# Gate and up as nine pairs of half-height matmuls in a two-layer SSM and GEGLU kernel

## The chip, the cores and the metric

The kernel runs on one core of a Trainium2 chip. The metric is device time in microseconds (us) for one execution; the time given for a kernel is the median of its runs. The engines are named as the profile names them: PE is TensorE (matmul; its weight loads are listed as PEld), DVE is VectorE, ACT is ScalarE, POOL is GpSimd and SP is SyncE, which issues most of the DMAs.

## The reference

The sequence x has 2048 rows of 576 channels (bf16). Two layers are applied, each made of a gated long convolution A and a feed-forward block B, both with a residual:

```
def _A_ref(q, k, v, shift_k, ssm_k, ssm_D):      # q is the normalised x
    kv = shift_conv(k, shift_k) * v              # 4 taps along the sequence
    y  = long_conv(kv, ssm_k) + kv * ssm_D       # causal, length 2048, by FFT
    return q * y
def _B_ref(x, w_gate, w_up, w_down):             # 576 -> 4608 -> 576
    return (_gelu(x @ w_gate) * (x @ w_up)) @ w_down

x = A_q
x = x + _A_ref(_layernorm(x), A_k, A_v, ...)
x = x + _B_ref(_layernorm(x), ...)
x = x + _A_ref(_layernorm(x), A_k, A_v, ...)
x = x + _B_ref(_layernorm(x), ...)
```

k, v and the filters are the same in both layers, so y is computed once. Only the normalisation, the product with y, and the feed-forward block are done per layer.

## The kernel before

The first part (function `ssm_phase_A`, lines 71 to 256) computes y by block-wise Fourier transforms on TensorE. Its filter transposes (L145) take five pieces of the 576 channels: four of 128 rows and one of 64.

The second part (`ssm_geglu_kernel`) holds the feed-forward block, and it is where the change is. The 2048 rows are cut into four chunks of CH = 512 rows, each of STC = 4 row tiles of 128. A *unit* is one chunk in one layer; L361 lists the eight units, all four chunks of layer 0 and then all four of layer 1. The hidden 4608 columns are cut into FT = 36 steps of 128, in nine groups of FG = 4 that share weight tiles. All weights stay in SBUF once loaded: group 0 is loaded in the first part (`load_w`, L325), groups 1 to 8 when the first part's buffers are free.

A unit, in the order in which it is written out (L434 on):

- `ln_finish` (L387) has transposed the normalised chunk: per block of 128 channels four transposes (L400) into a PSUM tile, then a copy to SBUF on DVE (L401). 576 is 4 x 128 + 64. The first four blocks serve gate and up alike. For the last 64 channels there are two extra blocks, `xnT_rA` with the 64 channels in its lower rows (rows 0 to 63) and zeros above, and `xnT_rB` with zeros below and the channels in its upper rows (64 to 127). The tile `wr` holds the last 64 rows of the gate weights in its lower half and those of up in its upper half, so a matmul of full height with `rA` gives gate's rest and one with `rB` gives up's.
- `gate_up(f)` (L438) runs five matmuls of 128 rows and 512 columns for gate into the PSUM tile pg, and then five for up into pu (L444, L447).
- `act_mul` (L451) applies GELU to pg on ACT (L453) and multiplies with pu on DVE (L455), which gives hT.
- `down(f)` (L458) multiplies hT with the down weights: for each of four row tiles one matmul of 512 columns (L461) and one of 64 (L464), accumulated in five PSUM banks (acc) over all 36 steps.

PSUM has three tiles (psum_gu, L357) for pg, pu and the transposes, which take turns, and one set of acc tiles. The text writes gate_up(f+1) ahead of down(f), so TensorE goes gate_up(f), down(f-1), gate_up(f+1), down(f).

Work for later units is hung into the steps as tasks (L468 on): the product with y for the next layer's or the next chunk's rows (`gate_A1_st`, `_gate_residual` L271), the normalisation of the next unit's chunk (`ln_st`, L372), and at last `ln_finish` for it. The residual additions (L413, L415) end a unit. All chunks of x are loaded to SBUF in float32 through POOL's queue ahead of the loop (L421), and stay there.

The framework's planner takes the instructions in this order, with costs of its own, lets an engine go on with a later instruction that is ready when the next one isn't, and fixes each engine's order before the kernel runs; on the chip each engine keeps to its list. It also sets the semaphores.

Of the kernel before, what the change touches and what calls it, by code (L numbers as in the profile page):

```python
# [11 lines left out]
ALU = mybir.AluOpType  # L12
F32 = mybir.dt.float32
BF16 = mybir.dt.bfloat16
# [3 lines left out]
P = 128  # L18
# [264 lines left out]
def ssm_geglu_kernel(ctx, tc, A_q, A_k, A_v, A_shift_k, A_ssm_k, A_ssm_D, B_x, B_w_gate, B_w_up,  # L283
                     B_w_down, out, debug=None):
    nc = tc.nc
    q2 = A_q[0]
    out2 = out[0]
    S, D = q2.shape
    F = B_w_gate.shape[1]
    NST = S // P  # L290
    CH = 512
    NCH = S // CH
    STC = CH // P
# [4 lines left out]
    NDTF = D // P  # L298
    DREM = D - NDTF * P
# [2 lines left out]
    DR = D - DM  # L302
    assert STC * DR <= 512
    EPS = 1e-5
    XW = D + (2 * DREM if DREM else 0)
# [7 lines left out]
    neghalf_t = persist.tile([P, 1], F32, name="neghalf_t")  # L313
    nc.vector.memset(neghalf_t[:], -0.5)

    wg, wu, wr, wd = {}, {}, {}, {}
    fw = FG * P

    def alloc_w(pool, g):
        wg[g] = pool.tile([P, NDTF, fw], BF16, name=f"wg{g}")  # L320
        wu[g] = pool.tile([P, NDTF, fw], BF16, name=f"wu{g}")
        wr[g] = pool.tile([P, fw], BF16, name=f"wr{g}") if DREM else None
        wd[g] = pool.tile([P, FG, D], BF16, name=f"wd{g}")

    def load_w(g):  # L325
        f0 = g * fw
        nc.sync.dma_start(out=wg[g][:], in_=B_w_gate[0:NDTF * P, f0:f0 + fw].rearrange("(dt p) f -> p dt f", p=P))
        nc.sync.dma_start(out=wu[g][:], in_=B_w_up[0:NDTF * P, f0:f0 + fw].rearrange("(dt p) f -> p dt f", p=P))
        if DREM:
            nc.sync.dma_start(out=wr[g][0:DREM, :], in_=B_w_gate[NDTF * P:D, f0:f0 + fw])  # L330
            nc.sync.dma_start(out=wr[g][DREM:2 * DREM, :], in_=B_w_up[NDTF * P:D, f0:f0 + fw])
        nc.sync.dma_start(out=wd[g][:], in_=B_w_down[f0:f0 + fw, :].rearrange("(ft p) d -> p ft d", p=P))

    pre = ctx.enter_context(tc.tile_pool(name="pre", bufs=1))
# [5 lines left out]
        return  # L340

    xc0pool = ctx.enter_context(tc.tile_pool(name="xc0", bufs=1))
    x_c = [xc0pool.tile([P, STC, D], F32, name="x_c0")]
# [4 lines left out]
    for c in range(1, NCH):  # L348
        x_c.append(xrpool.tile([P, STC, D], F32, name=f"x_c{c}"))
# [16 lines left out]
    def ln_begin(c):  # L366
        stt = LNState()
        stt.c = c
        stt.xns = [None] * STC
        return stt  # L370

    def ln_st(stt, j):  # L372
        st = stt.c * STC + j
        mv = small.tile([P, 2], F32, tag="mv")
        rstd = small.tile([P, 1], F32, tag="rstd")
        _ln_stats(nc, small, xs(st), D, eps_t, neghalf_t, mv[:], rstd[:], "l_")
        xn = xnp.tile([P, XW], BF16, tag=f"xn{j}", bufs=1)
        nc.vector.tensor_scalar(out=xn[:, 0:D], in0=xs(st), scalar1=mv[:, 0:1],
                                scalar2=rstd[:, 0:1], op0=ALU.subtract, op1=ALU.mult)
        if DREM:  # L380
            nc.gpsimd.memset(xn[:, D:D + DREM], 0.0)
            nc.vector.tensor_scalar(out=xn[:, D + DREM:XW], in0=xs(st)[:, D - DREM:D],
                                    scalar1=mv[:, 0:1], scalar2=rstd[:, 0:1],
                                    op0=ALU.subtract, op1=ALU.mult)
        stt.xns[j] = xn

    def ln_finish(stt):  # L387
        xns = stt.xns
        xnT = xnp.tile([P, NDTF, CH], BF16, tag="xnT")
        xnT_rA = xnT_rB = None  # L390
        blocks = [(dt * P, xnT[:, dt, :]) for dt in range(NDTF)]
        if DREM:
            xnT_rA = xnp.tile([P, CH], BF16, tag="xnT_rA", name="xnT_rA")
            xnT_rB = xnp.tile([P, CH], BF16, tag="xnT_rB", name="xnT_rB")
            blocks.append((NDTF * P, xnT_rA[:]))
            blocks.append((NDTF * P + DREM, xnT_rB[:]))
        for (c0, dst) in blocks:
            pt = psum_gu.tile([P, CH], BF16, tag="gu")
            for j in range(STC):
                nc.tensor.transpose(out=pt[:, j * P:(j + 1) * P], in_=xns[j][:, c0:c0 + P], identity=ident[:])  # L400
            nc.vector.tensor_copy(out=dst, in_=pt[:])  # L401
        return xnT, xnT_rA, xnT_rB

    def residual_adds(layer, c, acc):
        last_layer = layer == NLAYER - 1
# [11 lines left out]
            if last_layer:  # L417
                nc.sync.dma_start(out=out2[st * P:(st + 1) * P, :], in_=ob[:])

    for c in range(NCH):  # L420
        nc.gpsimd.dma_start(out=x_c[c][:],  # L421
                            in_=q2[c * CH:(c + 1) * CH, :].rearrange("(st p) d -> p st d", p=P))
    for j in range(STC):
        gate_A1_st(j)
    wpool = ctx.enter_context(tc.tile_pool(name="weights", bufs=1))
    for g in range(1, NFG):
        alloc_w(wpool, g)
        load_w(g)
    st0 = ln_begin(units[0][1])
    for j in range(STC):  # L430
        ln_st(st0, j)
    cur = ln_finish(st0)
    pending = []
    for ui, (layer, c) in enumerate(units):  # L434
        xnT, xnT_rA, xnT_rB = cur
        acc = psum_acc.tile([P, STC + (1 if DR else 0), 512], F32, tag="acc")

        def gate_up(f):  # L438
            g, fi = divmod(f, FG)
            pg = psum_gu.tile([P, CH], F32, tag="gu")  # L440
            pu = psum_gu.tile([P, CH], F32, tag="gu")
            for (pd, wm, rr) in ((pg, wg[g], xnT_rA), (pu, wu[g], xnT_rB)):
                for dt in range(NDTF):
                    nc.tensor.matmul(pd[:], lhsT=wm[:, dt, fi * P:(fi + 1) * P], rhs=xnT[:, dt, :],  # L444
                                     start=(dt == 0), stop=(dt == NDTF - 1 and not DREM))
                if DREM:
                    nc.tensor.matmul(pd[:], lhsT=wr[g][:, fi * P:(fi + 1) * P], rhs=rr[:],  # L447
                                     start=False, stop=True)
            return pg, pu

        def act_mul(pg, pu):  # L451
# [23 lines left out]
        if ui + 1 < len(units):  # L475
            nlayer, ncu = units[ui + 1]
            assert ncu != c or NCH == 1
            if ncu != c:
                nxt_state = ln_begin(ncu)
                fslot = max(fslot, 6)  # L480
                for j in range(STC):
                    if nlayer == 0:
                        tasks.setdefault(min(fslot, FT - 1), []).append(lambda j=j, ncu=ncu: gate_A1_st(ncu * STC + j))
                        fslot += 1
                    tasks.setdefault(min(fslot, FT - 1), []).append(lambda j=j, stt=nxt_state: ln_st(stt, j))
                    fslot += 1
                tasks.setdefault(min(fslot, FT - 1), []).append("finish")
# [25 lines left out]
        cur = nxt_cur  # L513
# [50 lines left out]
```

## Time and profile before

| What | Value |
|---|---|
| Median of three runs | 1129.36 us (1128.77 to 1131.19) |
| Profiled execution: span, first to last instruction | 1127.3 us |
| Between this span and the median | 2.1 us |
| PE busy | 96% of the span, 6464 matmuls |
| DVE busy | 45% |
| ACT busy | 24% |
| Mean granted TensorE clock | 0.986 |
| First matmul of the feed-forward part | 202.3 us |

The page gives the profiled execution by its span, and no other time of its own; what lies around it is worked out against the median. In the timeline each row gives the start, the length, the engine, the source line, the operation with its output and inputs, the shape of the array used (rows*columns, as 128*128) and that of the data, and how many instructions were merged in the row. Matmuls are pipelined: a row's length is longer than the slot that the matmul takes from the next, so slots are read from start to start. A time in brackets is idle time of the engine ahead of the row, with what ended it.

### The profile page before, as it was taken

The page shows a single profiled execution, that of the slowest core. Times are in us where ns is not written, and L with a number is a line of the kernel's source. Part 1 is how long each engine was busy: PE and PEld are TensorE (multiplying, and loading weights), DVE is VectorE, ACT ScalarE, POOL GpSimd, SP SyncE. Part 2 cuts the span into 40 slices and gives each one's busy share as a digit, 9 for nine tenths or more (in the row PEclk, how much of TensorE's full clock was granted, in tenths as well). Part 3 has the DMA queues.
Part 4 walks back from the last instruction along what each step waited for, and adds up shares of the span by engine and source line. Part 5 has one row for each costly group of instructions (what it writes and reads, how often), then busy time and mean ns, then how long its engine had stood idle before and what let it go on. Part 6 is the DMA issues. An engine that isn't in the chain of part 4 may idle for free.

```text
span 1127.3 us, 15633 instructions
## 1 busy us (share of the span) xinstructions
PE 1080.8 (96%) x6464; PEld 519.2 (46%) x6464; DVE 507.0 (45%) x1072; ACT 265.8 (24%) x503; POOL 53.0 (5%) x111
## 2 busy tenths in 40 slices
PE   5999994999999999999999999999999999999997
PEld 1544433444444444444444444444444444444443
DVE  5947999722276226942652255323232322232222
ACT  5875211111111111111111111111111111111111
POOL 0001002100011001200100000000000000000000
PEclk9999997899999999999999999999999999999999
DMA  7921004950000000000000000000000000000000
GB/s 221 293 75 43 1 1 116 339 175 1 1 1 1 1 1 1 1 1 1 1 1 1 1 1 1 1 1 22 1 1 1 22 1 1 1 22 1 1 1 22
DMA packets 33654, 38.73 MB, mean 34 GB/s; under 512 B 1845, under 2 KB 31408, under 8 KB 33584
## 3 DMA queue, kind: packets, MB, share of 16 engines
q1 hardware_dynamic: 31472, 33.03, 9.8%
q0 software_dynamic: 2112, 4.72, 1.4%
q8 instruction: 50, 0.82, 0.3%
q14 instruction: 20, 0.16, 0.0%
HBM read 33.02 MB, written 2.36 MB: 31 GB/s over the span
## 4 chain that ended last, share of the span: by engine, by line
PE 82%; DVE 11%; issue 3%; DMA 1%; ACT 1%; POOL 1%; SPq 1%; DVEq 0%; ACTq 0%; POOLq 0%
PE acc L461 21%; PE pg L444 20%; PE pu L444 20%; PE pg L447 5%; PE pu L447 5%; PE ps L134 3%; PE acc L464 3%; DVE pr L231 2%; PE ps L254 2%; DVE stats L264 2%; PE Yps L235 1%; DVE hT L455 1%; PE pt L400 1%; DVE t L276 1%; POOL rstd L268 1%
## 5 line engine op out<-in xcount | busy, mean ns | idle before, releaser
L455 DVE TENSOR_TENSOR hT<-ga,pu 128x512 bf16<-128x512 f32 x288 | 197.4, 686 | 558.7 <-PE pu L447 557.5
L453 ACT ACTIVATE ga<-pg 128x512 f32<-128x512 f32 x288 | 171.9, 597 | 740.3 <-PE pg L447 730.1
L461 PEld LDWEIGHTS <-hT 128*128 128x128 bf16 x1152 | 112.7, 98 | 138.9 <-DVE hT L455 6.3
L464 PEld LDWEIGHTS <-hT 128*128 128x128 bf16 x1152 | 112.9, 98 | 32.1
L268 POOL TENSOR_TENSOR rstd<-ve,neghalf_t 128x1 f32<-128x1 f32 x64 | 44.2, 696 | 372.3 <-DVE ve L267 370.5
L134 PEld LDWEIGHTS <-GF 128*128 128x128 bf16 x512 | 35.2, 101 | 49.9 <-issue 20.1
L134 PE MATMUL ps<-hT_blk,GF 128*128 128x512 bf16 (+1 forms) x256 | 38.9, 311 | 11.4 <-ACT Hf_0_237 L137 4.8
L235 PE MATMUL Yps<-pr,ident 128*128 128x512 bf16 (+1 forms) x180 | 45.7, 330 | 1.7 <-DVE pr L231 0.7
L254 PE MATMUL ps<-zb,GI 128*128 128x512 bf16 (+1 forms) x192 | 34.4, 289 | 6.9 <-DVE zb L245 3.8
L461 PE MATMUL acc<-wd_2381,hT 128*128 128x512 bf16 x128 | 36.8, 380 | 1.0 <-DVE hT L455 1.0
L461 PE MATMUL acc<-wd_2390,hT 128*128 128x512 bf16 x128 | 36.5, 380 | 0.0
L461 PE MATMUL acc<-wd_2372,hT 128*128 128x512 bf16 x128 | 35.7, 380 | 0.0
L461 PE MATMUL acc<-wd_74,hT 128*128 128x512 bf16 x128 | 35.7, 380 | 0.0
L461 PE MATMUL acc<-wd_2408,hT 128*128 128x512 bf16 x128 | 35.7, 380 | 0.0
L461 PE MATMUL acc<-wd_2399,hT 128*128 128x512 bf16 x128 | 35.7, 380 | 0.0
L461 PE MATMUL acc<-wd_2417,hT 128*128 128x512 bf16 x128 | 35.7, 380 | 0.0
L461 PE MATMUL acc<-wd_2426,hT 128*128 128x512 bf16 x128 | 35.7, 380 | 0.0
L461 PE MATMUL acc<-wd_2435,hT 128*128 128x512 bf16 x128 | 35.0, 380 | 0.0
L134 PE MATMUL ps<-kv_blk,GF 128*128 128x512 bf16 (+1 forms) x256 | 32.8, 286 | 2.1 <-DVE kv_blk L195 1.1
L444 PE MATMUL pg<-xnT,wg_71 128*128 128x512 bf16 x128 | 33.8, 387 | 0.0
L444 PE MATMUL pu<-xnT,wu_72 128*128 128x512 bf16 x128 | 33.3, 383 | 0.0
L444 PE MATMUL pg<-xnT,wg_2405 128*128 128x512 bf16 x128 | 32.9, 379 | 0.0
(204 smaller groups left out, 1771.9 us busy)
## 6 DMA issues: line engine op xcount, KB each, us to landing
kj<-in_A_k_dram SPq DMA_DIRECT2D x29, 288.0 KB, 4.0
v_t<-in_A_v_dram SPq DMA_DIRECT2D x8, 288.0 KB, 5.1
out_dram<-ob SPq DMA_DIRECT2D x16, 144.0 KB, 1.8
x_c_2292<-in_A_q_dram POOLq DMA_DIRECT2D x1, 1152.0 KB, 5.9
x_c_2305<-in_A_q_dram POOLq DMA_DIRECT2D x1, 1152.0 KB, 5.8
x_c_2306<-in_A_q_dram POOLq DMA_DIRECT2D x1, 1152.0 KB, 11.0
x_c_2307<-in_A_q_dram POOLq DMA_DIRECT2D x1, 1152.0 KB, 15.1
skb<-in_A_shift_k_dram SPq DMA_DIRECT2D x1, 576.0 KB, 6.8
```

Of the source, the lines that this page charges most:

```text
L134: nc.tensor.matmul(ps[:], lhsT=GF[:, kt, mt * P:(mt + 1) * P], rhs=src_blk[:, kt, d0:d0 + dw], start=(kt == 0), stop=(kt == KT_F - 1))
L231: nc.vector.tensor_tensor(out=pr[:], in0=kvf[:, ko:ko + HH, :], in1=hf[:, ho:ho + HH, :], op=ALU.mult)
L235: nc.tensor.matmul(Yflat[:, c0:c0 + cw], lhsT=idm[:], rhs=prf[:, c0:c0 + cw], start=(ti == 0), stop=(ti == n_terms - 1))
L254: nc.tensor.matmul(ps[:], lhsT=GI[:, kt, mt * P:(mt + 1) * P], rhs=zb[:, kt, :], start=(kt == 0), stop=(kt == KT_I - 1))
L264: nc.vector.bn_stats(out=stats[:, h, :], in_=x_ap[:, h * w:(h + 1) * w])
L268: nc.gpsimd.tensor_tensor(out=rstd_out, in0=ve[:], in1=neghalf_t[:, 0:1], op=ALU.pow)
L444: nc.tensor.matmul(pd[:], lhsT=wm[:, dt, fi * P:(fi + 1) * P], rhs=xnT[:, dt, :], start=(dt == 0), stop=(dt == NDTF - 1 and not DREM))
L447: nc.tensor.matmul(pd[:], lhsT=wr[g][:, fi * P:(fi + 1) * P], rhs=rr[:], start=False, stop=True)
L453: nc.scalar.activation(out=ga[:], in_=pg[:], func=ACT.Gelu_apprx_tanh)
L455: nc.vector.tensor_tensor(out=hT[:], in0=ga[:], in1=pu[:], op=ALU.mult)
L461: nc.tensor.matmul(acc[:, j, 0:DM], lhsT=hT[:, j * P:(j + 1) * P], rhs=wd[g][:, fi, 0:DM], start=(f == 0), stop=(f == FT - 1))
L464: nc.tensor.matmul(acc[:, STC, j * DR:(j + 1) * DR], lhsT=hT[:, j * P:(j + 1) * P], rhs=wd[g][:, fi, DM:D], start=(f == 0 and j == 0), sto ...
```

## The change

- The weights of gate and up lie in one tile per group, `wgu`, of nine blocks. Its lower 64 rows hold gate's weights, its upper 64 rows up's. The 576 channels are nine pieces of 64; block b pairs two of them, so that the transposed block of 128 channels has in its lower rows the piece for gate and in its upper rows the piece for up. Over the nine blocks, each of gate and up meets every piece once.
- `gate_up` runs, for each of the nine blocks, one matmul of 64 rows for gate from the lower rows and one of 64 rows for up from the upper rows, both of 512 columns, in turn into pg and pu: 18 instructions in place of 10.
- `ln_finish` transposes and copies nine blocks (128 channels each, overlapping by half) in place of six. The last one wraps round from the end to the start of the channels, so the normalised row tile carries its first 64 channels a second time at its end; the cleared 64 columns and the memset on POOL go.
- `load_w` loads each group with six DMAs of 64 partitions and the down weights', seven in all in place of five.
- The units go in another order: both chunks of a pair through layer 0, then both through layer 1, then the next pair. Only two buffers hold chunks of x. The first two chunks are loaded ahead of the loop, and the others at the start of the unit before the one that needs them, into a buffer given free.

```diff
+    HK = P // 2
+    NKC = D // HK
+    XW = D + HK
+    NXB = NKC
+    for b in range(NXB):
+        c0 = (b * P) if b < NDTF else ((b - NDTF) * P + HK if b < 2 * NDTF else NDTF * P)
+        lo_of[b] = c0 // HK
+        hi_of[b] = (c0 // HK + 1) % NKC
...
-        wg[g] = pool.tile([P, NDTF, fw], BF16, name=f"wg{g}")
-        wu[g] = pool.tile([P, NDTF, fw], BF16, name=f"wu{g}")
-        wr[g] = pool.tile([P, fw], BF16, name=f"wr{g}") if DREM else None
+        wgu[g] = pool.tile([P, NXB, fw], BF16, name=f"wgu{g}")
...
+        for (w, r0, of) in ((B_w_gate, 0, lo_of), (B_w_up, HK, hi_of)):
+            wv = w[:, f0:f0 + fw].rearrange("(k p) f -> p k f", p=HK)
...
+                nc.sync.dma_start(out=wgu[g][r0:r0 + HK, b:b + n, :], in_=src)
...
-    units = [(layer, c) for layer in range(NLAYER) for c in range(NCH)]
+    units = [(layer, c + i) for c in range(0, NCH, 2) for layer in range(NLAYER) for i in range(2)]
...
-            nc.gpsimd.memset(xn[:, D:D + DREM], 0.0)
...
+        nc.vector.tensor_scalar(out=xn[:, D:XW], in0=xs(st)[:, 0:HK],
+                                scalar1=mv[:, 0:1], scalar2=rstd[:, 0:1],
+                                op0=ALU.subtract, op1=ALU.mult)
...
+        xnT = xnp.tile([P, NXB, CH], BF16, tag="xnT")
+        blocks = [(lo_of[b] * HK, xnT[:, b, :]) for b in range(NXB)]
...
+    def load_x(c):
+        if c not in x_c:
+            pool, tag = ((xc0pool, "x_c0"), (xrpool, "x_c1"))[c % 2]
+            x_c[c] = pool.tile([P, STC, D], F32, name=f"x_c{c}", tag=tag)
         nc.gpsimd.dma_start(out=x_c[c][:],
                             in_=q2[c * CH:(c + 1) * CH, :].rearrange("(st p) d -> p st d", p=P))
...
-            for (pd, wm, rr) in ((pg, wg[g], xnT_rA), (pu, wu[g], xnT_rB)):
-                for dt in range(NDTF):
-                    nc.tensor.matmul(pd[:], lhsT=wm[:, dt, fi * P:(fi + 1) * P], rhs=xnT[:, dt, :],
-                                     start=(dt == 0), stop=(dt == NDTF - 1 and not DREM))
-                if DREM:
-                    nc.tensor.matmul(pd[:], lhsT=wr[g][:, fi * P:(fi + 1) * P], rhs=rr[:],
-                                     start=False, stop=True)
+            for b in range(NXB):
+                for (pd, r0) in ((pg, 0), (pu, HK)):
+                    nc.tensor.matmul(pd[:], lhsT=wgu[g][r0:r0 + HK, b, fi * P:(fi + 1) * P],
+                                     rhs=xnT[r0:r0 + HK, b, :], start=(b == 0), stop=(b == NXB - 1))
...
+                if ncu not in x_c:
+                    load_x(ncu)
                 nxt_state = ln_begin(ncu)
```

More of the change, by code (lines that the diff above doesn't have):

```diff
@@ L347, in ssm_geglu_kernel @@
     xrpool = ctx.enter_context(tc.tile_pool(name="xrest", bufs=1))
-    for c in range(1, NCH):
-        x_c.append(xrpool.tile([P, STC, D], F32, name=f"x_c{c}"))
+    x_c[1] = xrpool.tile([P, STC, D], F32, name="x_c1", tag="x_c1")
     def xs(st):
@@ L388, in ln_finish @@
         xns = stt.xns
[L389 to L396, printed above, removed]
+        xnT = xnp.tile([P, NXB, CH], BF16, tag="xnT")
+        blocks = [(lo_of[b] * HK, xnT[:, b, :]) for b in range(NXB)]
         for (c0, dst) in blocks:
@@ L401, in ln_finish @@
             nc.vector.tensor_copy(out=dst, in_=pt[:])
-        return xnT, xnT_rA, xnT_rB
+        return xnT
     def residual_adds(layer, c, acc):
@@ L434, in ssm_geglu_kernel @@
     for ui, (layer, c) in enumerate(units):
-        xnT, xnT_rA, xnT_rB = cur
+        xnT = cur
         acc = psum_acc.tile([P, STC + (1 if DR else 0), 512], F32, tag="acc")
```

27 lines of the change are left out of this document (14 added, 13 removed).

## The prediction

> **What bounds the kernel now.** I read the page first: span, busy shares, then the chain of waits.
>
> ```profile
> span 1127.3 us, 15633 instructions
> PE 1080.8 (96%) x6464; PEld 519.2 (46%) x6464; DVE 507.0 (45%) x1072; ACT 265.8 (24%) x503; POOL 53.0 (5%) x111
> PE 82%; DVE 11%; issue 3%; DMA 1%; ACT 1%; POOL 1%; SPq 1%; DVEq 0%; ACTq 0%; POOLq 0%
> ```
>
> TensorE is busy 96% of the span and carries 82% of the chain; from about 202 us on it is never idle for long. So a change to gate and up is worth what it takes from or adds to the sequence of matmuls. I therefore went to the timeline, TensorE only, at one undisturbed step f of the hidden dimension.
>
> ```profile
> 705.30 1.03 PE L444 MATMUL pg<-xnT,wg_2387 128*128 128x512 bf16 x4
> 706.17 0.38 PE L447 MATMUL pg<-xnT_rA,wr_2389 128*128 128x512 bf16 x1
> 706.38 1.03 PE L444 MATMUL pu<-xnT,wu_2388 128*128 128x512 bf16 x4
> 707.25 0.38 PE L447 MATMUL pu<-xnT_rB,wr_2389 128*128 128x512 bf16 x1
> 707.46 0.38 PE L461 MATMUL acc<-wd_2390,hT 128*128 128x512 bf16 x1
> ...
> 708.41 0.19 PE L464 MATMUL acc<-wd_2390,hT 128*128 128x64 bf16 x1
> 708.44 1.03 PE L444 MATMUL pg<-xnT,wg_2387 128*128 128x512 bf16 x4
> ```
>
> Read the starts, not the durations: a matmul's row is longer than the slot it takes. Ten matmuls of 512 columns from 705.30 to 707.46 are 2.16 us, 0.216 each; the eight down matmuls to 708.44 take 0.98. The step is 3.14 us with no gap. There are 8 units (2 layers, 4 chunks) of 36 steps: 288 steps, 904 us of the span.
>
> **The change part by part.** *The pairs.* Ten slots become nine pairs. If the two halves of a pair run at the same time, a step loses one slot: 288 x 0.216 = 62.2 us gained. No row of this trace shows two half-height matmuls side by side. The bounds are 0.216 us a pair (full overlap) and 0.432 (none). I take the overlap, since the two halves use other rows and other PSUM tiles, and keep the other end as a rival.
>
> *The lag in a pair.* The upper half is issued after its own weight load. The nearest rows are the 64-column matmuls, each with a load:
>
> ```profile
> 700.19 0.19 PE L464 MATMUL acc<-wd_2381,hT 128*128 128x64 bf16 x1
> 700.19 0.10 PEld L461 LDWEIGHTS <-hT 128*128 128x128 bf16 x1
> 700.22 0.38 PE L461 MATMUL acc<-wd_2381,hT 128*128 128x512 bf16 x1
> 700.22 0.10 PEld L464 LDWEIGHTS <-hT 128*128 128x128 bf16 x1
> 700.43 0.19 PE L464 MATMUL acc<-wd_2381,hT 128*128 128x64 bf16 x1
> ```
>
> A load and a matmul pass in 0.03 us (700.19 to 700.22), so the upper chain trails by 0 to 0.03 us. It trails once a step, not once a pair, as both chains then advance by 0.216. In the middle: 288 x 0.015 = 4.3 us lost (0 to 8.6). [...]
>
> *Changing the shape.* This kernel already holds half-height matmuls: the last 64 channels of the filter are transposed from 64 rows between transposes of 128.
>
> ```profile
> L145 PE MATMUL pt<-ident,hn_105 x20: 199/219/230, 42.1 to 43.8; 128*128 128x128 bf16 x16, 64*128 64x64 bf16 x4
> ```
> ```profile
> 42.10 1.90 PE L145 MATMUL pt<-ident,hn_105 128*128 128x128 bf16 x20
> ...
> 43.94 0.82 PE L134 MATMUL ps<-hT_blk,GF 128*128 128x512 bf16 x3
> ```
> ```profile
> 700.71 0.83 PE L400 MATMUL pt<-ident,xn 128*128 128x128 bf16 x12
> 701.38 0.38 PE L461 MATMUL acc<-wd_2381,hT 128*128 128x512 bf16 x1
> ```
>
> Twelve full-height transposes take 701.38 - 700.71 = 0.67 us, 0.056 each. So 16 of them are 0.89, and four of 64 columns at 0.03 are 0.11: 1.00 us. The twenty took 43.94 - 42.10 = 1.84. The 0.84 too much falls on eight changes between 128 and 64 rows: 0.105 us each, 0.21 for there and back. [...] After the change every step goes gate/up (64 rows), down (128 rows), and back: 0.21 us a step against the 0.216 saved. At a unit's start two gate/up groups stand side by side, so 35 round trips a unit: 280 x 0.21 = 58.8 us lost. This one term eats the gain.
>
> *Waits in a step.* Gate now ends with up, not five matmuls earlier, and three PSUM tiles serve both.
>
> ```profile
> 703.49 0.38 PE L447 MATMUL pg<-xnT_rA,wr_2389 128*128 128x512 bf16 x1
> 703.91 0.60 ACT L453 ACTIVATE ga<-pg 128x512 f32<-128x512 f32 x1 [4.46 <-PE pg L447]
> 704.57 0.38 PE L447 MATMUL pu<-xnT_rB,wr_2389 128*128 128x512 bf16 x1
> 705.08 0.68 DVE L455 TENSOR_TENSOR hT<-ga,pu 128x512 bf16<-128x512 f32 x1
> ```
>
> The GELU starts 0.42 us after the last gate matmul starts and runs 0.60, so the gate tile is free 1.02 us after that start, which is 0.80 after its slot. The next pair needs that tile as its second target, and comes after a shape change, 0.98 us of down and another change: 1.19 us. Covered by 0.39; without the two changes it would be covered by 0.18. VectorE's product (0.69) then ends 0.80 + 0.69 = 1.5 us after the pairs, and down needs it after 1.19 + 1.96 = 3.15: 1.6 us to spare. Before, it could start 0.2 us after up's last slot and was needed after 0.98 + 2.16: 2.2 us to spare. Behind a late product stand all of TensorE's later instructions. I take nothing; a crowded VectorE is a rival.
>
> *The normalised chunk.* Nine blocks are transposed and copied per unit instead of six.
>
> ```profile
> 701.13 1.42 DVE L401 COPY xnT<-pt 128x512 bf16<-128x512 bf16 x4 [0.44 <-PE pt L400]
> 701.61 0.71 PE L400 MATMUL pt<-ident,xn 128*128 128x128 bf16 x8
> 702.40 0.39 PE L400 MATMUL pt<-ident,xn 128*128 128x128 bf16 x4
> 702.63 1.03 PE L444 MATMUL pg<-xnT,wg_2387 128*128 128x512 bf16 x4
> ```
>
> Now the stage lasts 702.63 - 700.71 = 1.92 us, of which 0.47 is down work put between (the gaps between the three transpose rows and their 24 slots): 1.45 net. Twelve more transposes are 12 x 0.056 = 0.67 if TensorE sets the pace. If the copies do: four in 1.42 us are 0.355 each, the next gate tile waits for the seventh (0.42 + 7 x 0.355 = 2.9 us) with a product between (0.6), so 3.5, less at most 0.98 of down: 2.5, which is 1.05 more. I take 0.85: seven times in the loop 6.0 us, and three copies, 1.1, before the first unit. Sum 7.1 lost (5.8 to 8.5). The GpSimd clearing that goes cost nothing: other work lies beside it. The second normalising pass on DVE stays, 64 columns as before.
>
> *Weights.* Seven issues on SP's queue per group of four steps in place of five, the same bytes.
>
> ```profile
> 187.62 0.37 SPq L327 DMA_DIRECT2D wg_2369<-in_B_w_gate_dram  x1
> 234.80 0.37 SPq L332 DMA_DIRECT2D wd_2435<-in_B_w_down_dram  x1
> ```
>
> Eight groups are issued in 47.6 us, 5.9 a group; the steps eat a group in 12.5 us from 202 on. Were the two thirds that go to half the partitions at half the rate, a group would take 5.9 x 5/3 = 9.9: still ahead. Nothing; what hides it is the first unit.
>
> *The order of chunks.* Two chunks of x are loaded at the start, two in units 3 and 4 on GpSimd's queue, each behind the residual additions of the chunk whose buffer it takes; behind it in that queue stand the normalisation's powers, and VectorE behind those.
>
> ```profile
> x_c_2292<-in_A_q_dram POOLq DMA_DIRECT2D x1, 1152.0 KB, 5.9
> ```
> ```profile
> PEld L461 <- DVE hT L455: 6.3, 17, 0.9
> ```
>
> A load lands in 5.9 us; its readers come from slot 6 on, 18 us into the unit, unless they are put forward. 0 to 11.8 us for both, I take 1. In return a unit has at most eight row tiles of norm and gate work on VectorE, now twelve in units 1 and 2. TensorE waits for products 6.3 us in all; that may go (-6.3) or stay. I take no change.
>
> Sum: -62.2 + 4.3 + 58.8 + 7.1 + 1 = +9.0 us on a span of 1127.3: 1136.3. Around the span lie 1129.36 - 1127.3 = 2.1 us: **1138.4 us**. The terms' own bounds give 1129 to 1152.
>
> **The rivals.** *Entry is not paid (faster).* The change into 64 rows was priced where the new weights came right behind 128-row ones. If the first pair's weights can be loaded under the last down matmul, as the load at 700.22 is under its neighbour, entry falls away: 280 x 0.105 = 29.4 us less, 1109. It decides from about half of that price on, since the forecast is only 9 us above. Against it: both directions cost in the rows above, four groups alike. 0.14, from 1105 to 1127.
>
> *VectorE arrives in lumps (slower).* The instruction order is fixed beforehand by a planner with costs of its own. In a crowded stretch it lays as much norm work between two products as fits a step:
>
> ```profile
> 343.54 0.67 DVE L455 TENSOR_TENSOR hT<-ga,pu 128x512 bf16<-128x512 f32 x1
> ...
> 347.00 0.68 DVE L455 TENSOR_TENSOR hT<-ga,pu 128x512 bf16<-128x512 f32 x1
> ...
> 350.81 0.68 DVE L455 TENSOR_TENSOR hT<-ga,pu 128x512 bf16<-128x512 f32 x1
> ```
>
> Products 3.5 to 3.8 us apart, already more than a step of 3.14. If the planner counts eighteen halves one after another, its step is 18 x 0.216 + 0.98 = 4.87, and it lays 4.2 us between products. From rows like these a unit's residual, gate and norm work is some 20 us (an estimate): five products, 24 us, where TensorE wants 16; less the slack of 1.6, 6 us a unit, seven units, 42 us: 1180. It decides once its steps are over about 3.6 us. The trace can't show its costs. 0.18, from 1152 to 1185.
>
> *Weights uncovered.* [...] 0.06.
>
> *The halves don't run together*, so the change isn't what its words say: 288 x 9 x 0.216 = 560 us more, 1698. 0.06.
>
> **How the numbers follow.** Forecast 1138.4, chance 0.56, own range 1129 to 1152. The range 1120 to 1185 leaves out the last two rivals (0.12) and half of the faster one (0.07). Three timed runs spread by 0.2%, which is about what a measurement can tell from none: 1127.1 to 1131.6. Faster: 0.14. Same: the forecast's low edge, 0.10. Slower: 0.76.
>
> **What would show it.** Right: pairs starting within 0.03 us of each other and 0.216 after the last; about 0.105 us between the end of a slot and the next start at each change of shape (so about 0.32 from the last half-height start, 0.13 from the last 64-column start); a step of 3.15 to 3.17 us; 36 transposes in about 3.5 us. Wrong: a step below 3.10 (changes cheaper), products of VectorE ahead of idle TensorE (lumps), or a half starting only when the other ends.

## The result, and the profile after

The changed kernel takes 1198.62 us (median of four runs, 1197.96 to 1198.92) against 1129.2 for the kernel before (four runs, 1128.77 to 1131.19): ratio 1.0615, 95% interval 1.0602 to 1.0628. The direction was forecast, but the time lies above the forecast of 1138.4 and above the range's upper end, 1185. The page of the changed kernel, with the same three lines as before:

```profile
span 1197.1 us, 20266 instructions
PE 1085.8 (91%) x8706; PEld 483.7 (40%) x8864; DVE 518.4 (43%) x1096; ACT 265.5 (22%) x503; POOL 53.6 (4%) x79
...
PE 74%; DVE 14%; issue 5%; DMA 3%; POOL 2%; ACT 1%; SPq 1%; POOLq 0%; DVEq 0%; ACTq 0%
```

TensorE's busy time has hardly moved (1080.8 to 1085.8 us), yet its share of the span fell from 96% to 91%: the 69.8 us are mostly time in which TensorE stands still. On the chain of waits TensorE went from 82% to 74%, VectorE from 11% to 14%. So I looked first at a step with nothing else in it (timeline of TensorE, changed kernel; L454 is gate and up, L468 and L471 are down):

```profile
904.16 0.19 PE L471 MATMUL acc<-wd,hT 128*128 128x64 bf16 x1
904.29 0.39 PE L454 MATMUL pg<-xnT,wgu 64*128 64x512 bf16 x1
904.29 0.39 PE L454 MATMUL pu<-xnT,wgu 64*128 64x512 bf16 x1
904.51 0.38 PE L454 MATMUL pg<-xnT,wgu 64*128 64x512 bf16 x1
...
906.02 0.38 PE L454 MATMUL pg<-xnT,wgu 64*128 64x512 bf16 x1
...
906.34 0.39 PE L468 MATMUL acc<-wd,hT 128*128 128x512 bf16 x1
...
907.30 0.19 PE L471 MATMUL acc<-wd,hT 128*128 128x64 bf16 x1
907.42 0.39 PE L454 MATMUL pg<-xnT,wgu 64*128 64x512 bf16 x1
```

Here the prediction holds. The two halves of a pair start within 0.01 us (3 to 4 ns in the trace's own times); the pairs are 0.216 us apart (904.29 to 906.02 in eight). From the last pair's start to the first down matmul are 0.31 us, so 0.31 - 0.216 = 0.09 for the change to 128 rows; from the last 64-column start to the next pair are 0.12, less its 0.03, so 0.09 for the change back. The first slot behind each change is another 0.01 us longer (904.29 to 904.51 is over 0.22), which makes about 0.105 a change. The step is 3.13 us, as long as before (3.14): the slot that was saved is paid back in two changes of shape.

The loss is elsewhere. The view of waits of the changed kernel gives, per waiting group and what ended its wait, the sum, the count and the longest wait in us:

```profile
PEld L468 <- DVE hT L462: 62.1, 41, 4.2
...
DVE stats L264 <- DMA x_c<-in_A_q_dram: 8.9, 3, 4.0
```

Down's weight loads wait 62.1 us for VectorE's product (L462), where it was 6.3 before. VectorE's timeline in the second unit shows why:

```profile
334.81 0.68 DVE L462 TENSOR_TENSOR hT<-ga,pu 128x512 bf16<-128x512 f32 x1
335.40 0.81 DVE L278 SCALAR_TENSOR_TENSOR x_c<-t,rstd,x_c 128x576 f32<-128x576 f32 x1
...
339.51 0.81 DVE L276 SCALAR_TENSOR_TENSOR t<-x_c,mv,y_sb 128x576 f32<-128x576 f32 x1
340.24 0.68 DVE L462 TENSOR_TENSOR hT<-ga,pu 128x512 bf16<-128x512 f32 x1
...
345.68 0.68 DVE L462 TENSOR_TENSOR hT<-ga,pu 128x512 bf16<-128x512 f32 x1
...
350.48 0.68 DVE L462 TENSOR_TENSOR hT<-ga,pu 128x512 bf16<-128x512 f32 x1
```

The products are 5.4, 5.4 and 4.8 us apart, with gate and norm work between them, where a step of TensorE is 3.13. The same stretch on TensorE:

```profile
341.21 0.19 PE L471 MATMUL acc<-wd,hT 128*128 128x64 bf16 x1 [2.47 <-DVE hT L462]
...
342.07 0.39 PE L454 MATMUL pg<-xnT,wgu 64*128 64x512 bf16 x1
...
346.42 0.39 PE L468 MATMUL acc<-wd,hT 128*128 128x512 bf16 x1 [2.23 <-DVE hT L462]
...
348.17 0.60 PE L454 MATMUL pg<-xnT,wgu 64*128 64x512 bf16 x1
...
348.57 0.63 PE L454 MATMUL pg<-xnT,wgu 64*128 64x512 bf16 x1
...
349.00 0.63 PE L454 MATMUL pg<-xnT,wgu 64*128 64x512 bf16 x1
```

Two steps in a row end in a wait of 2.2 to 2.5 us, and the step from 342.07 to 348.17 is 6.10 us long. After the second wait the pairs are 0.43 us apart instead of 0.216 (348.57 to 349.00). That is the granted clock, as the windows of the changed kernel show (start and end, length, busy time and count of PE, PEld, DVE, ACT and POOL, granted clock, DMA share, GB/s):

```profile
338.00:342.00 4.00, 1.53 (x15) 0.62 (x12) 4.00 (x10) 0.60 (x1) 1.61 (x2) 1.00 0.00 0
342.00:348.00 6.00, 3.77 (x28) 1.45 (x26) 5.14 (x19) 0.60 (x1) 1.64 (x3) 0.90 0.00 0
348.00:352.00 4.00, 3.80 (x26) 1.44 (x26) 2.49 (x8) 0.60 (x1) 0.55 (x1) 0.73 0.00 0
```

VectorE is busy for the whole of the first window while TensorE stands most of it; then the mean granted clock of a window is 0.90 and 0.73.

Where the 69.8 us of span are, worked out from the starts of the gate/up groups, in us. A crowded step counts with what it is over 3.135, the median step; in the second unit, for instance, four steps of 3.99, 5.44, 6.10 and 4.13 are 7.1 over.

| Place | Change |
|---|---|
| Crowded steps of seven units: 5.7, 7.1, 7.2, 10.3, 11.0, 7.1, 7.3 over, 55.82 in all, before 2.27 | +53.6 |
| Steps with the transposes of the next chunk, over steady steps: 2.73 a unit, before 1.47; seven times | +8.8 |
| First steps of a unit, over steady steps: 1.14 in four units and 0.92 in three, before 0.06 | +6.9 |
| Start: the first gate/up at 200.8 instead of 202.3, its first two groups 9.47 instead of 6.83 | +1.1 |
| All other steps together | -0.8 |
| From the start of the last gate/up group to the end of the span: 11.2, before 10.95 | +0.2 |

That makes the 69.8.

### The profile page after: what moved, and what is told of

It reads as the page before. It is cut to its first block, busy times and chain, and to the rows that moved or that the text cites. A ratio compares the mean times of both kernels' runs of the same rounds, so it can differ in the third digit from the quotient of the medians.

```text
span 1197.1 us, 20266 instructions
## 1 busy us (share of the span) xinstructions
PE 1085.8 (91%) x8706; PEld 483.7 (40%) x8864; DVE 518.4 (43%) x1096; ACT 265.5 (22%) x503; POOL 53.6 (4%) x79
## 3 DMA queue, kind: packets, MB, share of 16 engines
q1 hardware_dynamic: 31760, 33.03, 11.6%
## 4 chain that ended last, share of the span: by engine, by line
PE 74%; DVE 14%; issue 5%; DMA 3%; POOL 2%; ACT 1%; SPq 1%; POOLq 0%; DVEq 0%; ACTq 0%
PE pg L454 41%; PE acc L468 18%; PE acc L471 4%; PE ps L134 3%; DVE stats L264 3%; PE pu L454 3%; DVE pr L231 2%; DVE x_c L278 2%; PE ps L254 2%; POOL rstd L268 2%; PE pt L404 1%; DVE hT L462 1%; PE Yps L235 1%; DMA x_c<-in_A_q_dram 1%; DMA kj<-in_A_k_dram 1%
## 5 line engine op out<-in xcount | busy, mean ns | idle before, releaser
L454 PE MATMUL pg<-xnT,wgu 64*128 64x512 bf16 x2592 | 620.7, 382 | 1.0
L454 PE MATMUL pu<-xnT,wgu 64*128 64x512 bf16 x2592 | 618.5, 382 | 0.4
L462 DVE TENSOR_TENSOR hT<-ga,pu 128x512 bf16<-128x512 f32 x288 | 197.2, 686 | 602.5 <-ACT ga L460 602.5
L454 PEld LDWEIGHTS <-wgu 64*128 64x128 bf16 x5184 | 242.0, 95 | 316.8 <-issue 84.9
L468 PE MATMUL acc<-wd,hT 128*128 128x512 bf16 x1008 | 292.8, 384 | 16.9 <-DVE hT L462 16.9
L471 PE MATMUL acc<-wd,hT 128*128 128x64 bf16 x1152 | 223.1, 194 | 49.1 <-DVE hT L462 20.9
L468 PEld LDWEIGHTS <-hT 128*128 128x128 bf16 x1152 | 112.7, 98 | 266.5 <-issue 104.5
L471 PEld LDWEIGHTS <-hT 128*128 128x128 bf16 x1152 | 113.5, 98 | 3.0 <-issue 3.0
L231 DVE TENSOR_TENSOR pr<-KVf,Hf 128x1024 bf16<-128x1024 bf16 (+1 forms) x160 | 62.2, 454 | 9.6 <-PE ps L134 5.7
L264 DVE BATCH_NORM_STATS2 stats<-x_c 128x6 f32<-128x288 f32 x128 | 52.5, 436 | 9.0 <-DMA x_c<-in_A_q_dram 8.9
L134 PE MATMUL ps<-hT_blk,GF 128*128 128x64 bf16 (+1 forms) x252 | 37.3, 302 | 12.3 <-ACT Hf L137 6.8
L134 PE MATMUL ps<-kv_blk,GF 128*128 128x64 bf16 (+1 forms) x252 | 32.6, 284 | 2.4 <-DVE kv_blk L195 1.1
L137 ACT ACTIVATE KVf<-ps 128x512 bf16<-128x512 f32 (+1 forms) x64 | 23.7, 411 | 11.4 <-PE ps L134 11.2
L278 DVE SCALAR_TENSOR_TENSOR x_c<-t,rstd,x_c 128x576 f32<-128x576 f32 x32 | 26.1, 814 | 0.1
```

The lines of the kernel that those rows point to most:

```text
L134: nc.tensor.matmul(ps[:], lhsT=GF[:, kt, mt * P:(mt + 1) * P], rhs=src_blk[:, kt, d0:d0 + dw], start=(kt == 0), stop=(kt == KT_F - 1))
L231: nc.vector.tensor_tensor(out=pr[:], in0=kvf[:, ko:ko + HH, :], in1=hf[:, ho:ho + HH, :], op=ALU.mult)
L264: nc.vector.bn_stats(out=stats[:, h, :], in_=x_ap[:, h * w:(h + 1) * w])
L278: nc.vector.scalar_tensor_tensor(out=x_out_ap, in0=t[:], scalar=rstd[:, 0:1], in1=x_in_ap, op0=ALU.mult, op1=ALU.add)
L454: nc.tensor.matmul(pd[:], lhsT=wgu[g][r0:r0 + HK, b, fi * P:(fi + 1) * P], rhs=xnT[r0:r0 + HK, b, :], start=(b == 0), stop=(b == NXB - 1))
L462: nc.vector.tensor_tensor(out=hT[:], in0=ga[:], in1=pu[:], op=ALU.mult)
```

## The experiments

My theory after the result: VectorE's lumps make the loss, and they come from the order that is fixed beforehand, not from the half-height matmuls as such. Rivals: the new order of chunks with its late loads; a cost of the half-height matmuls outside an undisturbed step. Where a ratio is given, it is against the kernel before, timed together with it on the same chip (1128.95, 1129.08 and 1128.55 us), with its 95% interval.

**The order of chunks alone.** The kernel before, with only the new order of units, two buffers for x and the late loads.

```diff
-    units = [(layer, c) for layer in range(NLAYER) for c in range(NCH)]
+    units = [(layer, c + i) for c in range(0, NCH, 2) for layer in range(NLAYER) for i in range(2)]
...
-    for c in range(NCH):
+    def load_x(c):
+        if c not in x_c:
+            pool, tag = ((xc0pool, "x_c0"), (xrpool, "x_c1"))[c % 2]
...
+                if ncu not in x_c:
+                    load_x(ncu)
```

> The kernel before with the new order of chunks and the two x buffers alone; full-height matmuls as before. Theory (most of the 69 us lost comes from VectorE's work laid in lumps between the products, because the planner takes the half-height matmuls as longer than they are): the planner's matmuls are unchanged here, so no lumps; 1125 to 1136 us, the late x loads costing at most some 7. Rival (the new order of chunks, its late loads and its crowding do the harm): 1170 to 1198.

It took 1128.78 us, ratio 0.9998 (0.9988 to 1.0007). As a whole the new order costs nothing here. Its view of waits has the wait for x as well,

```profile
DVE stats L264 <- DMA x_c<-in_A_q_dram: 5.5, 3, 2.3
```

but little is late behind it: in the fourth and fifth units four and three steps of up to 3.82 us are 1.7 and 1.2 over, and the first gate/up comes 2.7 us earlier (199.6 instead of 202.3). In the changed kernel the same wait (8.9 us) stands ahead of VectorE's lumps, in the fourth and fifth units, the two that are 10.3 and 11.0 over where the others are 5.7 to 7.3.

**VectorE's work spaced out, in the changed kernel.** Each task for a row tile is tied behind a step's product, one every third step.

```diff
+        todo = [x for s in sorted(tasks) for x in tasks[s]]
+        tasks = {}
+        s0 = 2 if ui and units[ui - 1][0] == 0 else 4
+        dist = min(3.0, (FT - 2 - s0) / max(1, len(todo)))
+        for i, x in enumerate(todo):
+            tasks.setdefault(int(s0 + i * dist), []).append(x)
...
-                    t()
+                    with tc.issue_after(mul.ins if hasattr(mul, "ins") else mul):
+                        t()
```

> The changed kernel, with the norm and gate work of one row tile tied behind the product of a step, one row tile every third step, so that the planner can't put it forward. Theory (lumps): the some 49 us in the crowded steps go, and most of the 7 us of waits for x; 1138 to 1152 us. What is left over the kernel before is the nine blocks and halves that run unpaired around them. Rival (half-height matmuls and shape changes cost it): unchanged, over 1185.

It took 1140.57 us, ratio 1.0103 (1.0088 to 1.0118): 58 us less than the changed kernel, from nothing but when VectorE's side work is issued; the transposes behind that work and the waits for x (8.9 us, now 1.3) move with it. VectorE's timeline of the spaced kernel:

```profile
335.43 0.69 DVE L462 TENSOR_TENSOR hT<-ga,pu 128x512 bf16<-128x512 f32 x1 [1.78 <-ACT ga L460]
338.56 0.69 DVE L462 TENSOR_TENSOR hT<-ga,pu 128x512 bf16<-128x512 f32 x1 [2.45 <-ACT ga L460]
...
341.64 0.82 DVE L278 SCALAR_TENSOR_TENSOR x_c<-t,rstd,x_c 128x576 f32<-128x576 f32 x1 [0.44 <-POOL rstd L268]
342.38 0.68 DVE L462 TENSOR_TENSOR hT<-ga,pu 128x512 bf16<-128x512 f32 x1
```

Between two products there is now the work of one row tile or none, and it is VectorE that waits (1.78 and 2.45 us ahead of a product, for ScalarE's GELU). Its view of waits for TensorE:

```profile
PEld L468 <- DVE hT L462: 4.0, 11, 0.6
```

62.1 us became 4.0.

**The same spacing in the kernel before**, with the same edit, to have a fair comparison.

> Control: the kernel before with the same spacing of the norm and gate work. Theory: it had only some 2 us of long steps in two crowded units, so 1125 to 1132 us. If spacing by itself were worth tens of us, it would fall below 1110.

It took 1122.2 us, ratio 0.994 (0.9925 to 0.9955), a little better than expected: the small lumps of the kernel before were worth 2.3 us, and its first gate/up now comes at 197.5 us instead of 202.3. So pairs without lumps cost 1140.57 - 1122.2 = 18.4 us.

**Lumps without half-height matmuls.** The kernel before, with the work of two row tiles put between two products and the next product held behind it.

```diff
+        for i, x in enumerate(todo):
+            tasks.setdefault(s0 + i // 2, []).append(x)
...
+            for i in lump:
+                tc.add_manual_dep(mul.ins, i.name,
...
+                    with tc.issue_after(mul.ins):
+                        t()
+                    lump += [i for i in nc.cur_bb.bb.instructions[mark:] if i.engine == mul.ins.engine]
```

> The kernel before, full-height matmuls, but VectorE's norm and gate work forced into lumps: two row tiles between two neighbouring products, and the next product held behind them. Theory (lumps alone do the harm, whatever the matmuls are): each lump makes its step about 5.2 us in place of 3.14, less the slack once a unit; some 42 us on the spaced kernel's 1122: 1150 to 1175. Rival (half-height matmuls are needed for the loss): under 1135.

It took 1192.85 us, ratio 1.056 (1.0542 to 1.0577): as slow as the changed kernel but for half a per cent, with gate and up untouched, and more than I had expected. VectorE's timeline of this kernel:

```profile
342.08 0.68 DVE L455 TENSOR_TENSOR hT<-ga,pu 128x512 bf16<-128x512 f32 x1
...
347.68 0.82 DVE L278 SCALAR_TENSOR_TENSOR x_c<-t,rstd,x_c 128x576 f32<-128x576 f32 x1 [0.44 <-POOL rstd L268]
348.41 0.68 DVE L455 TENSOR_TENSOR hT<-ga,pu 128x512 bf16<-128x512 f32 x1
...
355.03 0.68 DVE L455 TENSOR_TENSOR hT<-ga,pu 128x512 bf16<-128x512 f32 x1
```

Products 6.3 and 6.6 us apart. These lumps are larger than those of the changed kernel (4.8 to 5.4 apart), and in the sixth and seventh units they cost next to nothing, so that the two times lie so close is luck; what the run shows is that lumps alone are enough. Two things that I had not counted are in it: a lump holds VectorE's waits for GpSimd's powers (0.44 us here), and the granted clock falls here too, to a mean of 0.72 from 354 to 360 us.

**One pair only.** The kernel before, with only the last 64 channels as a half-height pair: eight full matmuls, then one pair, and five blocks to transpose instead of six.

```diff
-            for (pd, wm, rr) in ((pg, wg[g], xnT_rA), (pu, wu[g], xnT_rB)):
+            for (pd, wm) in ((pg, wg[g]), (pu, wu[g])):
...
+            for (pd, r0) in ((pg, 0), (pu, DREM)):
+                nc.tensor.matmul(pd[:], lhsT=wr[g][r0:r0 + DREM, fi * P:(fi + 1) * P], rhs=xnT_r[r0:r0 + DREM, :],
+                                 start=False, stop=True)
```

> The kernel before, with the last 64 channels alone as one pair of half-height matmuls (eight of full height and one pair a step: nine slots as in the change), five transposed blocks in place of six, old order of chunks. The same two changes of shape a step as in the changed kernel, but only ten matmuls a step for the planner to count. Theory (lumps): step about 3.13 us, no lumps, 1122 to 1134 us. Rival (shape changes or half-height matmuls do the harm): well over 1150.

It took 1131.99 us, ratio 1.0027 (1.0018 to 1.0037). The median step is 3.135 us again: one slot less, one round trip of shapes more. There are small lumps in the second and third units (steps up to 4.24 us, some 4.8 us over), and TensorE's waits for the product are 11.5 us instead of 6.3. I put that down to gate now ending just ahead of up, which no run separates:

```profile
PEld L458 <- DVE hT L452: 11.5, 22, 1.3
```

With the same spacing added to it:

> The kernel before with the spacing and with the last 64 channels alone as one half-height pair. Theory: the slot saved pays the two changes of shape, the five blocks instead of six save 0.23 us seven times, no crowding: 1116 to 1124 us, level with or just under the spaced kernel before (1122). Rival (the pair itself cost the 3 us that it lost without spacing): 1124 to 1128.

It took 1122.52 us, ratio 0.9943 (0.9928 to 0.9958), level with the spaced kernel before (0.994). So the small loss of one pair was VectorE's order as well.

**What is left of the 18.4 us.** Three tries on the spaced pairs. The first takes the halves strictly in turn, since at a unit's start the trace shows gate's halves ahead of up's.

```diff
+                    if prev is not None:
+                        tc.add_manual_dep(mm.ins, prev.name,
+                                          mybir.DependencyInfo(mybir.DependencyClass.NoSync, mybir.DependencyReason.DATA),
+                                          reason="pairs in turn")
+                    prev = mm.ins
```

> The spaced pairs, with gate and up matmuls held strictly in turn, so that the planner can't send one half ahead around the transposes and at a unit's start. Theory: the halves that run alone there cost some 0.4 us fifteen times; 1131 to 1138 us against 1140.6. Rival (holding them back makes TensorE wait for the PSUM tile instead): no change or slower, 1139 to 1148.

It took 1142.83 us, ratio 1.0124 (1.0109 to 1.0139): no gain. That doesn't settle the theory, for by the trace the order in turn saves nothing there. TensorE's timeline at the start of the third unit, first in the spaced pairs and then in this kernel (L455 is gate and up, L474 down):

```profile
435.70 0.39 PE L454 MATMUL pg<-xnT,wgu 64*128 64x512 bf16 x1
436.09 0.39 PE L468 MATMUL acc<-wd,hT 128*128 128x512 bf16 x1
...
438.92 0.81 PE L454 MATMUL pg<-xnT,wgu 64*128 64x512 bf16 x3
...
441.06 0.81 PE L454 MATMUL pu<-xnT,wgu 64*128 64x512 bf16 x3
```
```profile
435.05 0.39 PE L455 MATMUL pg<-xnT,wgu 64*128 64x512 bf16 x1
435.44 0.39 PE L474 MATMUL acc<-wd,hT 128*128 128x512 bf16 x1
...
439.11 0.37 PE L455 MATMUL pu<-xnT,wgu 64*128 64x512 bf16 x1 [0.47 <-ACT ga L466]
```

In both kernels one gate half of the new unit runs alone ahead of the old unit's last down, with a change of shape on either side. In the second group of the unit the spaced pairs let gate run two slots ahead of up; held in turn, TensorE waits 0.47 us instead, for the GELU that reads a gate tile and so frees it, which was the rival. Either way the two steps around a unit's start take 7.19 us where two steady ones take 6.27.

The second gives every third copy of a transposed block to ScalarE.

```diff
+            if bi % 3 == 2:
+                nc.scalar.copy(out=dst, in_=pt[:])
+            else:
+                nc.vector.tensor_copy(out=dst, in_=pt[:])
```

> The spaced pairs (1140.6), with every third of the nine block copies on ScalarE in place of VectorE. Theory (the nine copies, one after another on VectorE at 0.355 us each, hold the next gate and up back for about 1 us at each of seven stages, and the first for about as much): 1130 to 1137 us. Rival (the 36 transposes themselves set the stage's length): 1138 to 1142.

It took 1139.67 us, ratio 1.0097 (1.0082 to 1.0112), within the interval of the run without it. In the trace the two steps with the transposes take 8.98 us as before (8.99), so at these seven stages VectorE's copies are not the cost; only the first stage is shorter (the second unit starts at 316.9 us instead of 319.2).

The third takes the changes of shape out of the steps: down runs in half-height matmuls too. In a step, its lower rows go to two PSUM banks and its upper rows to the two others, and in the next step the other way round, with the products of this step and the last; each product waits for the down matmuls of the step before, so that the row groups keep to their turns.

```diff
+        def down(s, after=None):
+            ra, rb = (0, HK) if s % 2 == 0 else (HK, 0)
+            fs = [f for f in (s, s - 1) if 0 <= f < FT]
+            seq = []
+            for f in fs:
+                seq += [(f, ra, 0, 0), (f, rb, 2, 0), (f, ra, 1, 0), (f, rb, 3, 0)]
+            for f in fs:
+                seq += [(f, ra, j, 1) for j in range(STC)]
...
+                mm = nc.tensor.matmul(dst, lhsT=hTs[f][r0:r0 + HK, j * P:(j + 1) * P],
```

> The spaced pairs, with the down matmuls in halves as well, so that TensorE keeps to 64 rows within the steps and changes shape only around the transposes. In each step the lower rows take two row tiles' sums and the upper rows the other two, for this and the last step, and the next step the other way round, so that no PSUM bank is written from both row groups at once; the 64-column rests lie all on one side, 0.11 us a step longer than balanced. Theory (the two changes of shape a step cost 0.2 us, 59 us in all, and eat the slot saved): step 9 x 0.215 + 4 x 0.215 + 8 x 0.028 = 3.0 us against 3.135, 1098 to 1115 us. Rival (what I read as shape changes is something else between gate/up and down, as their waits): step unchanged, 1135 to 1150 us.

It took 1108.77 us, ratio 0.9821 (0.9806 to 0.9835). TensorE's timeline of this kernel (L483 is down):

```profile
700.76 1.17 PE L483 MATMUL acc<-wd,hT 64*128 64x512 bf16 x13
701.74 0.39 PE L454 MATMUL pg<-xnT,wgu 64*128 64x512 bf16 x1
...
703.70 1.20 PE L483 MATMUL acc<-wd,hT 64*128 64x512 bf16 x14
704.71 0.39 PE L454 MATMUL pu<-xnT,wgu 64*128 64x512 bf16 x1
```

From one gate/up group to the next are 2.97 us, and in the following step 2.94, instead of 3.135: 0.18 a step of the 0.21 that a round trip costs, with the 64-column matmuls now all on one side. Over 288 steps that is 52 us, of which 31.8 arrive (1140.57 to 1108.77). By the traces 17 us are lost again in seven units: the steps with the transposes take 1.4 us more over the steady ones than in the spaced pairs, and a unit's end, where this kernel has a group of down more, with the steps behind it 1.0 us more.

**Going on from there.** In that kernel a step's eight 64-column matmuls all lie in the same half of the rows, with nothing beside them. Next, those of every other step are put beside the following step's first up matmul.

```diff
+            if s % 2 == 0 and s + 2 < FT:
+                owed.append((s, rests, after))
+                return emit_down(s, seq, after, None)
...
+            if owed:
...
+                order = [(pu, HK, 0), None]
```

> Down in halves (1108.8), with the rests of every second step put beside the next step's first up matmul, so that neither row group runs alone. Theory: its step of 2.97 us still holds some 0.1 us in which one row group runs alone; nine slots of 0.215, four of 0.215 and four of 0.028 give 2.91: 1085 to 1100 us. Rival (the chip had already overlapped the lone side with the next step, and strict turns bring new waits): 1105 to 1120.

It took 1104.01 us, ratio 0.9778 (0.9762 to 0.9794), nearer to the rival than to the hope. The step itself came out as summed. Its length alternates, and two neighbours mostly take 5.84 to 5.85 us together, 2.92 each against 2.91 (TensorE's timeline of this kernel, the first matmul of three gate/up groups):

```profile
362.13 0.38 PE L470 MATMUL pu<-xnT,wgu 64*128 64x512 bf16 x1
...
365.16 0.38 PE L470 MATMUL pg<-xnT,wgu 64*128 64x512 bf16 x1
...
367.97 0.38 PE L470 MATMUL pu<-xnT,wgu 64*128 64x512 bf16 x1
```

The hope was wrong on the other side: the kernel without balancing had 2.955 on the mean, not 2.97, so there was less to gain. In the last unit, which has no side work, 35 steps take 104.2 us instead of 105.4; the units before, from the second on, gain 0.4 to 0.6 each. VectorE is hardly later than without balancing: in the views of waits, down's weight loads wait 16.3 us in all for its product, and 15.0 without. What keeps the units with side work from gaining as much as the last I did not trace. The last two runs add ScalarE's copies to the last two kernels.

> The balanced halves with a third of the block copies on ScalarE. Theory: as the balanced one less 4 to 9 us. Rival (copies not in the way): level with it.

> Down in halves without the balancing, with a third of the block copies on ScalarE. Theory: 4 to 9 us under 1108.8, so 1099 to 1105. Rival (copies not in the way): 1106 to 1110.

They took 1103.96 us, ratio 0.978 (0.9766 to 0.9795), level with the run without the copies; and 1105.58 us, ratio 0.9792 (0.9778 to 0.9807), between theory and rival, where the intervals with and without them touch. All four kernels with down in halves beat both the kernel before and the changed one; the best are 2.2% below the kernel before.

## Why the prediction was wrong

The step that failed is "Waits in a step", in its last words: "I take nothing; a crowded VectorE is a rival." The rival happened. I had the sign, the place and the mechanism of it, and gave it 0.18.

- *The pairs* (62.2 us gained): right, 0.216 us a pair.
- *The lag in a pair* (4.3 lost): close to the lower bound. Up's half starts 3 to 4 ns behind gate's in an undisturbed step, some 1 us in all.
- *Changing the shape* (58.8 lost, 0.105 each way): right. Single rows give 0.09 between the slots and 0.01 on the first slot behind, and taking the round trip out gave 0.18 a step, 0.21 with the 64-column matmuls evened out. The runs show how long a change takes, not what the array does in it. The rival with a free entry is out, as entry costs as much as exit (0.09 us between the slots for each). With the three terms together a step came out at 3.13 us instead of the 3.15 to 3.17 foreseen.
- *The normalised chunk* (7.1 lost): right in kind, mis-sized: 8.8 in the loop, where I had put 6.0, and 1.1 at the start. The 36 transposes shown below took 3.17 us from first to next pair, where I had said about 3.5.

```profile
259.71 0.86 PE L404 MATMUL pt<-ident,xn 128*128 128x128 bf16 x12
...
262.88 0.39 PE L454 MATMUL pg<-xnT,wgu 64*128 64x512 bf16 x1
```

- *Weights* (nothing): right. A group is now issued in 8.3 us instead of 5.9, still ahead of the 12.5 in which the steps eat one, and TensorE waits 0.2 us in all for them to land. TensorE's loads of weights into the array stay hidden under half-height matmuls, since pairs run at 0.216 us; the rival of uncovered weights is out.
- *The order of chunks* (1 lost): right alone (ratio 0.9998), wrong in company. The readers of x were put forward, to 7 us into the unit, which the prediction had left open; VectorE then waits 3.7 and 4.0 us for x with a product behind, and these two units lose some 3 to 4 us more than the others.
- *Waits in a step* (nothing): wrong. I worked out 1.6 us to spare for a product that VectorE takes up at once, and then let that stand for stretches in which it has other work queued ahead. Measured: 53.6 us in crowded steps; 58 us come back when the same work is spaced.
- *The rival's price* (42 us): too low. I took 6 us a unit from the number of products only. The crowded steps were 5.7 to 11.0 us a unit: 4.2 us of work between products was the right size (4.8 to 5.4 apart), but waits for x and a lowered clock came on top. The mean granted clock fell from 0.986 to 0.974, so (0.026 x 1197.1) - (0.014 x 1127.3) = 15 us of clock were lost more than before; how much of that lies in time that TensorE would have waited for VectorE anyway isn't separated. From the rival's 1180.4 to 1198.6 are 18.2 us. The large parts are 11.6 of price (53.6 against 42), 6.9 in the units' first steps, which I had not foreseen, and 2.8 at the transposes and the start (9.9 against 7.1). The steady steps (0.8 gained where the three terms had lost 0.9) and the loads of x (1, which the 53.6 hold) take 2.7 off; the other -0.4 lies in the end of the span and around it.
- *The bounds.* As given, those of the single terms add up to 1125.5 to 1154.9 us, not to 1129 to 1152; it changes nothing here.

Settled by runs: the lumps are enough for a loss of this size without any half-height matmul (1192.85 us), and without lumps the pairs stand at 1140.57, 2.2 us from my forecast. Part of that nearness is luck, as the same spacing also took 6.8 us from the kernel before. Nor do half-height matmuls and changes of shape bring lumps by themselves: one pair a step has both changes, and without spacing it lost 3 us.

Open: why the planner lays more between products here. That it counts eighteen halves one after another (a step of 4.87 us by my sum) fits products 4.8 to 5.4 us apart, but its costs were not seen. Open too is how to win back the 18.4 us between spaced pairs and the spaced kernel before. By the traces 4 lie at the start (first gate/up at 201.7 instead of 197.5), whose cause I did not find, and 14 in the units (a unit's period is 116.5 instead of 114.5, seven times). Of these 2.0 a unit, 0.9 lie around the unit's start: the lone gate half with its two changes of shape takes 0.49, and the group in which gate runs two slots ahead of up 0.43. Another 1.3 lie at the transposes: twelve more of them are 0.67, and the rest fits one more round trip of shapes (0.21) and a group in which gate again runs some two slots ahead; 0.1 is gained in the steady steps. That is read from rows; no run took it away. That a gate/up group which needs two PSUM tiles at once waits for the last one to come free shows in the 0.47 us above. Down in halves with both row groups on one PSUM bank was not tried.

## What to carry to other kernels

A change to the bottleneck engine's instructions can leave each undisturbed step as it was (3.13 us here, before 3.14) and still lose several per cent (the ratio was 1.0615), because the order of the other engines is fixed beforehand; look at the crowded stretches, and tie side work to the steps by hand before judging the change (that alone gave 58 us back). Half-height pairs ran fully side by side here (0.216 us a pair), but each change between 64 and 128 rows cost about half a matmul of 512 columns (0.105 of 0.216 us), so nine pairs for ten matmuls paid only when what stands next to them kept the same shape (1108.77 us with down in halves; with down at full height 1140.57, against 1122.2 for the kernel before, all three spaced). Price a late producer with everything that may stand in its queue, and look at the granted clock behind the waits of TensorE (here 0.50 for 3.4 us behind waits of 2.16 and 2.23 us).

## What the runs showed of the hardware that I had not expected

- Behind a single wait of some 2.2 us the granted clock was 0.50 for 3.4 us, in which matmuls of 512 columns came 0.43 us apart instead of 0.216. The windows below show it twice in the changed kernel, each time the 3.4 us with the wait (2.23 and 2.16 us) and the 3.4 us behind. The clock fell to 0.50 seven times in that kernel's feed-forward part before its last 5 us, six times for 3.4 us and once for 6.8, each time behind 3.4 us in which TensorE was busy for at most 39%. In the first part of the kernel before, it also fell behind 3.4 us with TensorE busy for 61% and 51% (at 181.5 and 188.3 us). And behind the wait of 2.47 us that ended at 341.21 in the changed kernel the clock stayed at 1.00 up to 346.74, so the traces show no sharp limit, neither of the busy share nor of the length of a wait.

```profile
343.33:346.74 3.41, 1.18 (x11) 0.40 (x8) 2.91 (x10) 0.60 (x1) 0.78 (x2) 1.00 0.00 0
346.74:350.16 3.42, 3.42 (x18) 1.17 (x18) 2.30 (x8) 0.00 (x0) 1.09 (x2) 0.50 0.00 0
220.44:223.86 3.42, 1.32 (x11) 0.61 (x13) 2.00 (x4) 0.58 (x1) 0.55 (x1) 1.00 1.12 210
223.86:227.27 3.41, 3.41 (x18) 1.06 (x14) 0.00 (x0) 0.00 (x0) 0.00 (x0) 0.50 1.11 210
```

- A pair's lag is 3 to 4 ns in an undisturbed step and does not grow along nine pairs. Where up starts later (at the transposes, 0.12 us behind gate), the pairs still go on at 0.216 us.
- The change of shape costs about 0.1 us in either direction, behind matmuls of 512 and of 64 columns alike; only behind the lone gate half at a unit's start it is 0.17 (0.39 us from its start to the next, less the slot).
- Down's accumulation was split over the two halves of the rows, which wrote different PSUM banks at a time; a step then has no change of shape at all, and is 2.955 us on the mean, or 2.92 with the 64-column matmuls evened out.
